# Loose softmax for the first quads, and masks on GpSimd, in a fused attention and feed-forward kernel

## The chip, the cores and the metric

The kernel runs on one core of one Trainium2 chip. Times are device microseconds of an execution; the profile is one execution taken by the hardware profiler. A core has a matrix engine (TensorE, PE in the profile, with its weight loads as PEld), VectorE (DVE), ScalarE (ACT), GpSimd (POOL) and SyncE (SP, which issues most transfers). The engines run side by side, each takes its own instructions in order, and they wait for each other by semaphores.

## The reference, cut to what matters

Attention over 8 batches of 8 heads, 576 rows and 64 columns a head, in which each row keeps only scores within tau = 0.02 of its maximum. Then a feed-forward layer whose hidden value is the largest of three products.

```python
scores = scale * np.matmul(q, k.transpose(0, 1, 3, 2))
thresh = np.max(scores, axis=-1, keepdims=True) - tau
scores = np.where(scores >= thresh, scores, -1000000000.0)
scores = scores - np.max(scores, axis=-1, keepdims=True)
attn = np.exp(scores)
attn = attn / (np.sum(attn, axis=-1, keepdims=True) + 1e-09)
x = np.matmul(attn, v)                      # then heads side by side: 4608 x 512
h = np.maximum(np.maximum(x @ w1, x @ w2), x @ w3)   # 512 -> 768
return h @ w_out                            # 768 -> 512
```

## The kernel before, in words

Four heads of one batch make a quad; there are 16. A quad's score rows are worked in 9 chunks of 128 rows by two heads, so that a chunk is a tile of 128 x 1152, made of two half tiles of 128 x 576. In all there are 144 chunks and 288 half tiles. q and k are loaded in float32, turned by TensorE (`transposed`, letter T), copied out by ScalarE (queries, letter a) and mostly VectorE (keys, letter c); a copy of the queries with the partition halves exchanged is made mostly by GpSimd (`swapped`, letter q).

For each half tile, `scores` (S) puts 576 columns into one of four slots of PSUM. `maximum` (m) on VectorE moves them to a tile z and takes each row's maximum with it. What follows depends on the half tile's digit in the table `MASKED` (line 24):

- 0: `threshold` (s) computes maximum minus tau on VectorE. `exponents` (e) on ScalarE applies a parametric ReLU that leaves scores below the threshold as they are and flattens those above by 2^-100. `numerators` (n) on ScalarE takes exp with the scale 2^100 and adds up the row. So ScalarE passes over the half tile twice.
- 1: ScalarE takes exp once (e), and VectorE compares, multiplies and adds up (`numerators`, letter k).
- 2 and 3: like 0 and 1, but ScalarE reads the scores from PSUM and not from z.

Then VectorE takes the reciprocal of both row sums (`reciprocals`, r), GpSimd multiplies z by it into the bfloat16 tile P (`normalized`, p, one half tile at a time), and SyncE issues a transposing transfer of P (`turned`, t). Once a quad's nine chunks are turned, `product` (O) multiplies by v: two pieces per quad, each for two heads, in tiles of 128 x 64 of the matrix engine, 20 matmuls a piece for an unsplit batch. One piece is copied out to x by VectorE (w), the other by ScalarE (x). v is cast to bfloat16 by GpSimd (`cast_v`, y).

The feed-forward part of a batch (`ffn`; F, with its second half as B) makes 18 hidden products, three for each of six blocks of 128 hidden columns. ScalarE copies out the first (h), VectorE takes the maximum with the others (v). Output products follow; their results are copied out (u, f, j) and stored (o, i, d). Weights are loaded (g) and cast by GpSimd (z). Batch 7 is worked in two parts (`SPLIT`, line 38).

No planner runs in the kernel. The string `ORDER` (line 40) gives the order: each letter issues one step, a digit behind S, T, O, F or N names the PSUM slot. `_Ordered` makes each engine keep that order. So a wait of one step holds back all later steps on its engine.

Of the kernel before, what the change touches and what calls it, by code (L numbers as in the profile page):

```python
# [24 lines left out]
220202110002002100110000100020020312000112012010100000000010100000001100  # L25
001000111010000101100000000000110001100000011110110200100000100010000000
110001101110100100010000001001100100000100101111102300000100100000001000
001000110100100001000000000100100001011110100011011100002100001000001013
# [7 lines left out]
PBUFS = 6  # L36

SPLIT = {7: ((0, 1), (2, 3, 4))}

ORDER = """  # L40
lllllllllT0laqqlcT1aS2lcqqgmS0S3lemS1lmnT2lmeS3lsaS0mnqlqemT3lyerclcapsnS1lS2eqmlS3qemznmS2perS1mnpsmnpT3ske
ytS1erkpT2agmnT3pclesqS2aqetS0meqlrnspmS1eqsT2nmpS3tnrcS0zlemS2eprmS3npmtS0npsgS1sermpS2emyS3eptmT0eplmS1ayl
meS0kynS2tssT3snkynkercperlT3pmnpmntqremS0lasprgeT3pmeS2psstnplnS0mzecesqrmS3etqkeS2gpnmS1npsmtnS0prmleS3pmS
2npsmnS0yrsmetperS2epmO1eqtnkplemnzswT2teS3rplS1empnmS3tpnssrS1klepS0mapermtS2epmT1S3nmqtnkO2qemncpS3txrskT1
peS2rmeS0ptmegpamS2npS1ertsmpnlkzS2elmS3eS0mpnlO1srkepsmnO2tyeprgwnpmT1xS3cpeS0sszmF2eS1meBqkF0ngqT3shrsmBay
S2tvpnF3rpemS1BpemF0pnsvT2BnyctS1esrlsT2mphS3lezS1maF0myntpT2sS3ngrcqF1eBmpnS2svpBnrmS3peS0tmeyF2zmnF3lBsvep
S0rhkBptesF2mgeS1zvF0nsmBpteBsrgvpnF1kS3phS2semBnqmF0S3evqF2ntrmBpelS1spvBnlmS3qhF0rsmepS1tnBpsmS3ezvS2eS1rm
pF0etsyO3mnlkngpO2eswetkBxrmpT3nF2rvpaS1BnqmS0hspS3meF2prS1smntBzesmF3ezvT0tBeclT1yS2pnvS0apsmtS3eyrmlS1epS2
mepF0mnqsmnS3tkBnkeF1restpkumeS2prtBumlperkpS0ustS2umS3pesmS1eqtT0mO2nlpceqsrmO3ntywelkS0pxlS1meF3prnS2smBye
myF0thpskS1oeBpF2nlvF3nlrmBpeBkpS1hstsvS0eF3lrmpnF2mBepBsveF1nT0vBtarkS3lhqS2smleF0prF1mnBysntBveS2plvnS0pom  # L50
F3nyS1pmeBsysmF0thT2rrlpeS1clF3epsmBnqT2svBaS1evqS2nmF0pS3nmqBtnmT2pS1hrcpS3esmS0petF2melS1rmpBnF3skpetF0sve
BlBmnF2vhtF1esrBkpnS0vtT3npBmS2arvpS0ermO3eqtsmepT1swntpS0cF2epesmtnS3kT1nS0mtBessrkpameS3preS1mS0uqmuS3mpnS
1tsmS2pnoS0rempS3lempO1lnkqlemO2lnymeO0srkpetkeF3swxykxpT2BercnprtS1uyS2upmF0termqS3eBymN2lhsskpelkS0eF3ertm
S1pjBlmeS0plvF2npS1mnyF3tpmnBsopT0nvBaS1kF2ieqrssmS0hlpBmelT1qF3snrvF0epcBlepS2vBnpsmtS1nS3rmphS2mnpF1smeS0B
snmF3tevS2T0mF1atBrsekpBevS0thS2pmF3nymS1qeBrsmnpS0tvF2eplF1rmnpBskeBptF3hsvS0eBrsstpmnS1lvT2qeO0mpnlscnT3wS
1etF2srramS0lnqBmlF3eqvT1nBcpS0thF2pemS1perS3mpBnmS0ptesO1smpnkteF3yvxT0BraktyS2esS1vpeS0mpnS3meqF2mnyrmpnT0
S1lceBqmeptrskS0pulS3muS1epmS2teF0rmplnskpeS1mtO3eklekO2esrmpesBknpwxS1kutS2urmopS3nF0myeS1mBetpsmF2hlS3rkep
BlmnF0S1prnsvT3tepBmF2apsssvS1eBtqmeS0qrS3hmtS1epsmF2lnpF0mleF3koBnBrvpeBstyvS1phsS2nmF3emS0nrS1tpmBnprS2smn
F0pveF1pBsremT3ptevBpS2chF0tnmF3ekBT1nvS2aBsmlnF0qvS1eS2rtrespmS3eBmqF1hmpT2nBcpS3ekpT2O0sasvterlmpO2ekqntwS
3xklpS1eF2ssmnF0yrBnmyS3evBptemS1plhS2ssmT3eyF0rcpeF1mBpntT3vnByS2ravpS0nmtpS3nsmS1eF2srmpektepS3slmnS0Bmeqn  # L60
mT1ktuS3urS0lcpeO2rlmpelmpeO3klpelweF1kqnsxS0rkepS2tmS3eBymemepS0kuF3quT2smeBtrF1kphoS0aBmnpS3tsN2rnvplnmpS1
erkpF0tjsF3mnBpsseBvS2ihrS1pmelS0mqeF3S2mnytBpmnoS1rF0eprsvF2ntpmBeBvqF1htskpS3esS0rmetS2pnmF3pBnmF0pesvT2te
BcF1nsBrvpntBskphT2F3erS0vlapBmnF1qvS2etpBmT0hS3rscpnF2lmS1qesS0sempBemS3yF1nvtS0nmBnT2ssrmpO3etspveF0wnS1rk
BpaS3tmhS2elqsF1mlS0qnmS3ermpBF2espsmS0npvBeS3tmeS1rvpO0ntmnsmS2yxS3empF0eskyerT1mpeS2cBtnypsmelkS3ulS2muS1e
smT0O3nsrplnpO2awetmeF3rkpxseT0S1ycntS2meF0poBrnsmpnkpF1ukBurS2shBqemF3oepvS0lS2nsmqF1emBptBnvF0hrrS2speS3mp
F1emBpntT2vepF3BssaktS0nvlBemS2hS1rsmptF0nS3mpeBmtnT2F1svnF3cetBBsrnvpS2hsrqS0meS1pmeT3F2sprmaS0npBmeF3ptsvn
S1qS0mnBtqmeS2yF1prevS0epssBmnS3qmS2htpmF0nlF1keBsmBertvO3pnvepF0serwpT2nBcpF3hktS1eBsrsmpnT0S2vtpaS1remqT3S
0nmyF2qectT1BpasmS3epvS1nS0mqnF2rmpemtpT3eS1keqS0smBercntpS1mupS3emF0ukessS1rmtpnBmopkS2uskS1eO3rukekO0yxeO3
ynwtprmopS0xmpS2emF3peS1mteBrsmpS0nF2pmhtS1nkBS3evF0nstmN2erkpeF1mBjpsBevS2hskF0eF3rkpteBmF1nBpveBkO2hsrvpeS
0rtwS1pnmF2npmS3eBympF1ntrvS0epBmpS2rF3svtpeS0mnpS1sBmiF2smhF0ntkBBervpS1etF3smpnF2BervpS1hsBpnmF0tevS3F1nmB  # L70
etrBkpO2vhO3nspS1xrwepS0mpF3smS2etF1snmBeBstvnS2S0veS3meF1snkeF2rmpnmpeBnkBerrptukpuO3rN1xpuO0jpuO3wptF1xpF2
hF0tvF1vF3hF0vtF1vF2hF0viF1vF2ohF0voF1vF3hF2vF1vF3hF2vO1vO0wF2xF3F1huF0vF3vF2ohF1vF3vF2hF0vF1vF3hF0vF2vF3hF1
vF2vF0hF1vF2vF0uF1ouN0ofjdi
# [31 lines left out]
def kernel(  # L105
# [44 lines left out]
    def weight_loads():  # L150


        def piece(dst, src):
            my = {}

            def load():
                my["t"] = stage.tile([128, 4 * 256], F32, name="stage")
                sync.dma_start(out=my["t"].rearrange("p (k f) -> p k f", k=src.shape[1]), in_=src)

            def cast():  # L160
                pool.tensor_copy(out=dst, in_=my["t"].rearrange("p (k f) -> p k f", k=src.shape[1]))
# [12 lines left out]
    zz = ctx.enter_context(tc.tile_pool(name="zz", bufs=ZBUFS))  # L174
    pp = ctx.enter_context(tc.tile_pool(name="pp", bufs=PBUFS))
# [68 lines left out]
    vrs = [one.tile([128, 4, D], BF16, name=f"vr{x}") for x in range(3)]  # L244

    def cast_v(L):
        L["vb"] = vp.tile([128, 4, 4, D], BF16, name="vb")
        pool.tensor_copy(out=L["vb"], in_=L["vm"])
        yield
        L["vrb"] = vrs[(2 * L["b"] + L["qd"]) % 3]  # L250
        for r in range(2):
            rows = slice(64 * r, 64 * r + 64)
            pool.tensor_copy(out=L["vrb"][rows, 2 * r:2 * r + 2], in_=Ls[2 * L["b"]]["vr"][rows, 4 * L["qd"] + 2 * r:4 * L["qd"] + 2 * r + 2])
# [93 lines left out]

    def masked(g, idx, r):
        return by_mask[2 * number[g, idx] + r] in "13"
# [37 lines left out]

    def numerators(c, r):
        z, acc = c["z", r], c["sm"][:, r:r + 1]
# [10 lines left out]
    def normalized(c):  # L400
        c["P"] = P = pp.tile([128, W], BF16, name="P")
        for n in range(2):
            pool.tensor_scalar(out=P[:, n * S:(n + 1) * S], in0=c["z", n],
                                    scalar1=c["rs"][:, n:n + 1], scalar2=1.0, op0=OP.mult, op1=OP.mult)
            if n:
                line["t"].append(c)
# [383 lines left out]
    x = 0  # L790
# [39 lines left out]
```

## Time and profile before

| | |
|---|---|
| median of 3 runs | 442.17 us (441.26 to 442.67) |
| span of the profiled execution | 440.2 us (its run time is not listed apart from the runs above) |
| busy PE, DVE, ACT, POOL | 418.9, 393.9, 403.6, 317.0 us |
| granted TensorE clock, mean | 0.988 |
| normalizations on POOL | 288 (250 from z tiles at 819 ns, 38 from stage tiles at 783 ns) |
| first feed-forward product starts | 71.3 us |
| last feed-forward maximum starts | 431.8 us |

In the group rows a line holds the engine, the operation, the tile written and those read, the shape, a count, the busy time and the mean of one. All recorded operations have the line of one helper, so groups are told apart by tile names: sc are scores in PSUM, z the half tiles in SBUF, th and nm the threshold and maximum of a row, rs the reciprocals, ptq the turned P, o the products, xt the attention output x, ph and po the hidden and output products, tp the turned q and k.

### The profile page before, as it was taken

How to read it: one execution, taken by the hardware profiler on the slowest of the kernel's cores; microseconds unless marked ns; L12 is line 12 of the kernel's file. 1: busy time of each engine (PE TensorE's matmuls, PEld its weight loads, DVE VectorE, ACT ScalarE, POOL GpSimd, SP SyncE). 2: the span in 40 equal slices, each digit the busy share in tenths (PEclk: the TensorE clock that was granted, in tenths of full speed). 3: DMA queues.
4: the chain of work that ended last, by engine and by line, in shares of the span. 5: the costliest groups of instructions: out<-in, count | busy, mean ns of one | idle time of the engine just before them, and what ended most of it. 6: DMA issues, size and time to landing. Idle time of an engine off the chain costs nothing.

```text
span 440.2 us, 14283 instructions
## 1 busy us (share of the span) xinstructions
PE 418.9 (95%) x5188; PEld 313.6 (71%) x5190; DVE 393.9 (89%) x1248; ACT 403.6 (92%) x834; POOL 317.0 (72%) x420
## 2 busy tenths in 40 slices
PE   7696789999999999999999999999999999999996
PEld 6353446787788776787678777887688777786873
DVE  4888899999999999999999999999889999998542
ACT  4999999999999999999999999999999998989521
POOL 1988999998787778867786778886585776554400
PEclk9987999999999999999999999999999999999999
DMA  6999999999999999999999999999698778583812
GB/s 190 276 239 214 270 215 260 263 252 252 220 277 224 237 165 242 291 160 232 189 242 238 202 182 273 192 199 208 135 237 153 147 109 185 102 169 72 192 50 85
DMA packets 213959, 88.50 MB, mean 201 GB/s; under 512 B 189184, under 2 KB 202240, under 8 KB 213888
## 3 DMA queue, kind: packets, MB, share of 16 engines
q1 hardware_dynamic: 213360, 86.96, 95.4%
q8 instruction: 41, 0.67, 0.6%
q10 hardware_dynamic: 528, 0.62, 0.5%
q14 instruction: 30, 0.25, 0.2%
HBM read 35.65 MB, written 9.44 MB: 102 GB/s over the span
## 4 chain that ended last, share of the span: by engine, by line
PE 78%; DVE 5%; POOL 5%; issue 4%; ACT 3%; DMA 2%; SPq 1%; DVEq 0%; POOLq 0%; ACTq 0%
PE ph L93 31%; PE sc L93 26%; PE po L93 10%; PE o L93 8%; POOL P L93 4%; PE tp L93 3%; ACT z L93 3%; DVE z L93 3%; DMA qm<-in_q_dram 2%; SPq L93 1%; DVE kt L93 1%; POOL w L93 1%; DVE stage L93 0%; DVE hm L93 0%; POOL qs L93 0%
## 5 line engine op out<-in xcount | busy, mean ns | idle before, releaser
L93 POOL TENSOR_SCALAR P<-z,rs 128x576 bf16<-128x576 f32 x250 | 202.0, 819 | 59.1 <-DVE rs L93 30.4
L93 DVE TENSOR_SCALAR_CACHE_REDUCE z<-sc 128x576 f32<-128x576 f32 x250 | 183.2, 749 | 12.2 <-PE sc L93 8.1
L93 PE MATMUL sc<-kt,qs 64*128 64x256 f32 (+2 forms) x640 | 179.8, 417 | 5.5 <-DVE z L93 3.9
L93 PE MATMUL sc<-kt,qt 64*128 64x320 f32 (+2 forms) x640 | 180.9, 429 | 3.1 <-DVE z L93 1.2
L93 PE MATMUL ph<-xt,w 64*128 64x288 bf16 (+2 forms) x2160 | 172.0, 283 | 0.2 <-DVE hm L93 0.2
L93 PEld LDWEIGHTS <-w 64*128 64x128 bf16 (+1 forms) x2160 | 128.0, 94 | 31.6 <-issue 4.0
L93 ACT ACTIVATE z<-z,th 128x576 f32<-128x576 f32 x161 | 120.5, 767 | 2.2 <-DVE th L93 1.9
L93 ACT ACTIVATE z<-z 128x576 f32<-128x576 f32 x175 | 117.6, 674 | 0.2
L93 PEld LDWEIGHTS sc<-kt,qs 64*128 64x128 f32 (+1 forms) x640 | 92.4, 179 | 22.5 <-DVE z L93 8.6
L93 PEld LDWEIGHTS sc<-kt,qt 64*128 64x128 f32 (+1 forms) x640 | 92.0, 179 | 14.7 <-DVE z L93 3.5
L93 DVE SCALAR_TENSOR_TENSOR z<-z 128x576 f32<-128x576 f32 x75 | 61.7, 827 | 1.4 <-ACT z L93 1.1
L93 POOL COPY qs<-qt 64x640 f32<-64x640 f32 (+3 forms) x66 | 45.9, 695 | 19.5 <-ACT qt L93 16.1
L93 ACT ACTIVATE z<-z,nm 128x576 f32<-128x576 f32 x72 | 53.9, 767 | 0.0
L93 PE MATMUL po<-wo,hT 64*128 64x512 bf16 (+3 forms) x454 | 53.3, 354 | 0.3
L93 DVE TENSOR_TENSOR hm<-ph,hm 128x576 bf16<-128x576 f32 (+2 forms) x54 | 37.0, 685 | 9.8 <-PE ph L93 9.6
L93 ACT ACTIVATE hm<-ph 128x576 bf16<-128x576 f32 (+2 forms) x54 | 31.9, 590 | 14.3 <-PE ph L93 13.8
L93 PEld LDWEIGHTS <-hT 64*128 64x128 bf16 (+2 forms) x456 | 28.4, 95 | 18.5 <-issue 2.6
L93 DVE TENSOR_TENSOR hT<-ph,hm 128x576 bf16<-128x576 f32 (+2 forms) x54 | 36.9, 683 | 2.8 <-PE ph L93 1.0
L93 PE MATMUL o<-ptq,vb 128*64 128x512 bf16 (+2 forms) x544 | 38.7, 282 | 0.2 <-DVE z L93 0.2
L93 POOL TENSOR_SCALAR P<-stage,rs 128x576 bf16<-128x576 f32 x38 | 29.5, 783 | 11.7 <-DVE rs L93 8.4
L93 ACT ACTIVATION_READ_ACCUMULATOR z<-z 128x1 f32 x175 | 33.6, 192 | 0.0
L93 PEld LDWEIGHTS <-vb 128*64 128x64 bf16 x544 | 22.4, 111 | 14.0 <-issue 5.6
(44 smaller groups left out, 412.2 us busy)
## 6 DMA issues: line engine op xcount, KB each, us to landing
vm<-in_v_dram SPq DMA_DIRECT2D x32, 256.0 KB, 4.6
qm<-in_q_dram SPq DMA_DIRECT2D x15, 512.0 KB, 4.7
km<-in_k_dram SPq DMA_DIRECT2D x15, 512.0 KB, 5.4
out_dram<-ob SPq DMA_DIRECT2D x14, 512.0 KB, 4.5
stage<-in_moe_w_dram SPq DMA_DIRECT2D x9, 512.0 KB, 5.6
ptq<-P SPq DMA_TRANSPOSE x144, 4.5
vr<-in_v_dram SPq DMA_DIRECT2D x16, 128.0 KB, 3.8
stage<-in_moe_w_out_dram SPq DMA_DIRECT2D x3, 512.0 KB, 5.5
```

The lines of the kernel that those rows point to most:

```text
L93: ins = fn(*a, **kw)
```

## The change

It has four parts, and a new order text.

- **Loose quads.** For the first three quads (`LOOSE = 3`), exp or the mask writes straight to P in bfloat16, without row sums, reciprocal and normalization. Instead TensorE makes a third product per quad with a matrix of ones in the place of v, which gives each head's row sums on 32 partitions. ScalarE takes their logarithm (L) and the exponential of its negative (E). VectorE multiplies both product pieces by that on the way to x (`scaled`, on w).
- **Masks on GpSimd.** 34 half tiles have the digit 4. After `threshold`, GpSimd computes (threshold minus score) times 2^100 and writes it as a saturated int8 into the high byte of a bfloat16 tile (`marked`, b): a huge number where the score is below the threshold, nothing or minus zero elsewhere. GpSimd adds this to z (`moved`, C), and ScalarE takes exp once (G). 13 of them lie in the first three quads.
- **Products in 32-column tiles.** A piece now holds the even or odd columns of all four heads, in four tiles of 128 x 32, 40 matmuls a piece for an unsplit batch. v is cast in that layout, and the rows of the hidden weights are loaded in the matching order, in two transfers each.
- **Buffers.** v has two buffers instead of three, P keeps six, now as named tags, one mark tile is added, the 9th-row output tile is shared with the logarithms, and the activation set with log and exp is asked for at the start.

Digits 0 to 4 of the table: 187, 84, 14, 3, 0 before and 162, 80, 10, 2, 34 after.

```diff
-MASKED = """ 2202021100020021001100001000200203...
+MASKED = """ 4201042142001321424220142114041004...
-ORDER = """ lllllllllT0laqqlcT1aS2lcqqgmS0S3lem...
+ORDER = """ lllllllllllT1lT0aclqqacqqS1lS2lmS0l...
+FARS = 1
+LOOSE = 3
+FAR = 2.0 ** 100
...
+                    for qd in range(2):
+                        sync.dma_start(out=my["t"].rearrange("p (qd j f) -> p qd j f", qd=2, j=2)[:, qd], in_=src[:, qd])
...
-                yield piece(t[:, :, cols], w[:, cols].rearrange("(ko p) f -> p ko f", p=128))
+                yield piece(t[:, :, cols], w[:, cols].rearrange("(qd p j) f -> p qd j f", qd=2, j=2))
...
-    vp = ctx.enter_context(tc.tile_pool(name="vp", bufs=3))
+    vp = ctx.enter_context(tc.tile_pool(name="vp", bufs=2))
...
-        pool.tensor_copy(out=L["vb"], in_=L["vm"])
+        pool.tensor_copy(out=L["vb"].rearrange("p h c j d -> p (h c) j d"),
+                         in_=L["vm"].rearrange("p h c (d j) -> p (h c) j d", j=2))
...
+        if on_pool(c, r):
+            if loose(c["g"]):
+                scalar.activation(out=part_of(c, r), in_=z, func=AF.Exp, bias=c["nm", r], scale=-1.0)
+            else:
+                scalar.activation(out=z, in_=z, func=AF.Exp, bias=c["nm", r], scale=-1.0, accum_out=summed(c)[:, r:r + 1])
+            return
...
+    def marked(c, r):
+        c["far", r] = t = far[next(fars) % FARS]
+        pool.tensor_scalar(out=t.bitcast(mybir.dt.int8).rearrange("p (n x) -> p n x", x=2)[:, :, 1],
+                           in0=c["z", r], scalar1=c["th", r], scalar2=FAR, op0=OP.add, op1=OP.mult)
+
+    def moved(c, r):
+        pool.tensor_tensor(out=c["z", r], in0=c["z", r], in1=c["far", r], op=OP.add)
...
+        if loose(c["g"]):
+            if masked(c["g"], c["idx"], r):
+                vector.scalar_tensor_tensor(out=part_of(c, r), in0=z, scalar=thr, in1=z, op0=OP.is_ge, op1=OP.mult)
+            else:
+                scalar.activation(out=part_of(c, r), in_=z, func=AF.Exp, scale=-1.0 / FLAT)
+            return
...
-                for i in range(2):
-                    w = vb[:, 2 * r + i, (1, 3, 0, 2)[m], :] if m < 4 else vrb[:, 2 * r + i, :]
-                    tensor.matmul(ps[64 * i:64 * i + 64, p0:p0 + n], w,
+                for h in range(4):
+                    r, i = divmod(h, 2)
+                    if j is None:
+                        w = ones[2 if m < 4 else r]
+                    else:
+                        w = vb[:, h, (1, 3, 0, 2)[m], j, :] if m < 4 else vrb[:, h, j, :]
+                    tensor.matmul(ps[32 * h:32 * h + 32, p0:p0 + n], w,
...
+        def logs():
+            L["rec", part] = hp_.tile([128, S], F32, name="ob9", bufs=1)
+            scalar.activation(out=L["rec", part][:, 0:hi - lo], in_=source(), func=AF.Ln)
+
+        def inverses():
+            t = L["rec", part][:, 0:hi - lo]
+            scalar.activation(out=t, in_=t, func=AF.Exp, scale=-1.0)
+
+        def scaled():
+            vector.tensor_tensor(out=dest(), in0=source(), in1=L["rec", part][:, 0:hi - lo], op=OP.mult)
...
+    if LOOSE:
+        scalar.preload_act_table_set("natural_log_exp_and_others")
...
-                    for r in range(2):
-                        yield product(Ls[g], r, x_of, part)
+                    for j in (None, 0, 1) if loose(g) else (0, 1):
+                        yield product(Ls[g], j, x_of, part)
```

More of the change, by code (lines that the diff above doesn't have):

```diff
@@ L74 @@
+d
 """
@@ L242, in load @@
                 yield
-    vrs = [one.tile([128, 4, D], BF16, name=f"vr{x}") for x in range(3)]
+    vrs = [one.tile([128, 4, 2, D // 2], BF16, name=f"vr{x}") for x in range(3)]
     def cast_v(L):
-        L["vb"] = vp.tile([128, 4, 4, D], BF16, name="vb")
-        pool.tensor_copy(out=L["vb"], in_=L["vm"])
+        L["vb"] = vp.tile([128, 4, 4, 2, D // 2], BF16, name="vb")
+        pool.tensor_copy(out=L["vb"].rearrange("p h c j d -> p (h c) j d"),
+                         in_=L["vm"].rearrange("p h c (d j) -> p (h c) j d", j=2))
         yield
@@ L400, in normalized @@
     def normalized(c):
-        c["P"] = P = pp.tile([128, W], BF16, name="P")
+        c["P"] = P = paper(c)
         for n in range(2):
@@ L413, in turned, with product @@
         sync.dma_start_transpose(out=L["pt"][:, :, c["idx"] * 128:(c["idx"] + 1) * 128], in_=c["P"])
-    def product(L, r, target, part=None):
+    ones = [one.tile([128, D // 2], BF16, name=f"ones{x}") for x in range(3)]
+    vector.memset(ones[2], 1.0)
+    for x in range(2):
+        vector.memset(ones[x], 1.0)
+        vector.memset(ones[x][64 - 64 * x:128 - 64 * x], 0.0)
+    def product(L, j, target, part=None):
         pt, vb, vrb = L["pt"], L["vb"], L["vrb"]
@@ L678, in chunks @@
             made.append(c)
+            if not loose(g):
+                tight.append(c)
             yield c
@@ L753, in issue @@
         elif what == "s":
-            threshold(*line["s"].pop(0))
+            c, r = line["s"].pop(0)
+            threshold(c, r)
+            if on_pool(c, r):
+                line["b"].append((c, r))
+        elif what == "G":
+            exponents(*line["G"].pop(0))
+        elif what == "b":
+            c, r = line["b"].pop(0)
+            marked(c, r)
+            line["C"].append((c, r))
+        elif what == "C":
+            c, r = line["C"].pop(0)
+            moved(c, r)
+            line["G"].append((c, r))
         elif what == "e":
@@ L757, in issue @@
             exponents(c, r)
[L758 removed]
+            if True:
+                line["k" if masked(c["g"], c["idx"], r) else "n"].append((c, r))
         elif what in "nk":
             c, r = line[what].pop(0)
[L761 to L764 removed]
             numerators(c, r)
         elif what == "r":
[L767 removed]
+            c = tight[line["r"].append(0) or len(line["r"]) - 1]
             assert c["summed"]
```

164 lines of the change are left out of this document (91 added, 73 removed).

## The prediction

> **What bounds the kernel now.** I read the page's busy times and slices first, then the chain, then windows cut at the first matrix product of the feed-forward part (71.3 us), then waits, then the instruction groups ahead of that cut.
>
> ```profile
> span 440.2 us, 14283 instructions
> PE 418.9 (95%) x5188; PEld 313.6 (71%) x5190; DVE 393.9 (89%) x1248; ACT 403.6 (92%) x834; POOL 317.0 (72%) x420
> PE   7696789999999999999999999999999999999996
> ACT  4999999999999999999999999999999998989521
> PE 78%; DVE 5%; POOL 5%; issue 4%; ACT 3%; DMA 2%; SPq 1%; DVEq 0%; POOLq 0%; ACTq 0%
> ```
>
> PE is full except at both ends; ACT is full from the second slice on. So two different bounds follow one another. The windows (length, then busy us and count of PE, PEld, DVE, ACT, POOL, then granted clock and DMA) part them:
>
> ```profile
> 0.00:8.40 8.40, 6.47 (x69) 5.73 (x71) 2.48 (x11) 2.38 (x4) 1.73 (x8) 1.00 0.59 149
> 8.40:71.30 62.90, 48.51 (x436) 28.11 (x434) 55.45 (x188) 62.00 (x132) 56.29 (x74) 0.92 1.14 246
> 71.30:85.00 13.70, 13.13 (x184) 9.95 (x182) 12.47 (x41) 13.37 (x30) 12.61 (x19) 1.00 1.18 265
> 85.00:400.00 315.00, 314.60 (x4145) 244.03 (x4147) 302.98 (x961) 307.71 (x630) 240.01 (x314) 1.00 1.01 204
> 400.00:440.20 40.20, 36.16 (x365) 25.74 (x363) 20.50 (x52) 18.12 (x41) 6.30 (x8) 1.00 0.39 101
> ```
>
> ```profile
> PE ph L93 <- DVE hm L93: 0.2, 1, 0.2
> ```
>
> From 8.4 to 71.3 ACT is busy 62.00 of 62.90 us and PE only 48.51, at a clock of 0.92: softmax paces, PE starves. From 85 to 400 PE is busy 314.60 of 315.00, and the single wait above is all it has there: PE paces. So work taken from ACT after 85 us buys nothing; what counts is when PE becomes full, and that is near the first feed-forward product.
>
> **The first stretch, engine by engine.** Groups from 0 to 71.3 us (count, then total busy us, mean ns, idle before):
>
> ```profile
> L93 ACT ACTIVATE z<-z 128x576 f32<-128x576 f32 x36 | 24.2, 674 | 0.0
> L93 ACT ACTIVATE z<-z,th 128x576 f32<-128x576 f32 x26 | 19.6, 767 | 0.6 <-DVE th L93 0.3 <-DVE rs L93 0.2
> L93 ACT ACTIVATE z<-z,nm 128x576 f32<-128x576 f32 x12 | 9.2, 766 | 0.0
> L93 ACT ACTIVATE z<-sc,nm 128x576 f32<-128x576 f32 x12 | 8.7, 728 | 1.3 <-DVE z L93 1.3
> L93 ACT ACTIVATION_READ_ACCUMULATOR z<-z 128x1 f32 x36 | 6.9, 193 | 0.0
> L93 ACT ACTIVATE qt<-tp 128x640 f32<-128x640 f32 (+3 forms) x10 | 5.4, 542 | 2.2 <-PE tp L93 1.9 <-DVE kt L93 0.2
> L93 ACT ACTIVATE xt<-o 128x576 bf16<-128x576 f32 x2 | 1.3, 631 | 0.0
> L93 DVE TENSOR_SCALAR_CACHE_REDUCE z<-sc 128x576 f32<-128x576 f32 x53 | 38.7, 751 | 6.7 <-PE sc L93 4.2 <-POOL P L93 2.3
> L93 DVE SCALAR_TENSOR_TENSOR z<-z 128x576 f32<-128x576 f32 x12 | 10.0, 843 | 0.3 <-ACT z L93 0.2
> L93 DVE COPY kt<-tp 128x640 f32<-128x640 f32 (+3 forms) x9 | 5.8, 650 | 0.0
> L93 DVE TENSOR_SCALAR th<-nm 128x1 f32<-128x1 f32 x28 | 3.8, 146 | 0.1
> L93 DVE RECIPROCAL rs<-sm 128x2 f32<-128x2 f32 x23 | 3.6, 158 | 0.8 <-ACT z L93 0.7
> L93 POOL TENSOR_SCALAR P<-z,rs 128x576 bf16<-128x576 f32 x46 | 35.8, 791 | 3.0 <-DVE th L93 1.4 <-POOL vr L93 0.9
> L93 POOL COPY qs<-qt 64x640 f32<-64x640 f32 (+3 forms) x16 | 10.3, 646 | 9.4 <-ACT qt L93 8.7
> L93 POOL CAST w<-stage 128x1024 bf16<-128x1024 f32 x6 | 6.7, 1120 | 0.1
> L93 POOL CAST vb<-vm 128x1024 bf16<-128x1024 f32 x3 | 3.1, 1035 | 0.1
> L93 POOL CAST vr<-vr 64x128 bf16<-64x128 f32 x5 | 3.0, 600 | 0.1
> ```
>
> Instructions overlap, so a mean is more than what each takes from its engine. The timeline (start, length) gives the step from one start to the next:
>
> ```profile
> 51.30 0.77 ACT L93 ACTIVATE z<-z,nm 128x576 f32<-128x576 f32 x1
> 51.96 0.68 ACT L93 ACTIVATE z<-z 128x576 f32<-128x576 f32 x1
> 52.53 0.20 ACT L93 ACTIVATION_READ_ACCUMULATOR z<-z 128x1 f32 x1
> 52.63 0.73 ACT L93 ACTIVATE z<-sc,nm 128x576 f32<-128x576 f32 x1
> 53.25 0.78 ACT L93 ACTIVATE z<-z,th 128x576 f32<-128x576 f32 x1
> 51.79 0.75 DVE L93 TENSOR_SCALAR_CACHE_REDUCE z<-sc 128x576 f32<-128x576 f32 x1
> 52.58 0.15 DVE L93 TENSOR_SCALAR th<-nm 128x1 f32<-128x1 f32 x1
> 52.65 0.75 DVE L93 CAST xt<-o 128x576 bf16<-128x576 f32 x1
> ```
>
> ACT: biased exponential or flattening 0.66, plain exponential 0.57, reading its sum 0.10, flattening from PSUM 0.62; other ACT groups are taken at mean less 0.10. DVE: group mean less 0.07 or 0.08, so maximum 0.68, threshold 0.07.
>
> **The sum to the first feed-forward product.** I count the letters of the order text ahead of its first F, old against new, and the mask kinds among them.
>
> ACT. Old: 38 first passes from SBUF x 0.66 + 12 from PSUM x 0.62 + 36 second passes x (0.57 + 0.10) + query copies 4.4 + 2 product copies x 0.53 = 62.1, against 62.00 busy. New: 29 x 0.66 + 9 x 0.62 + 24 x 0.57 (loose, no sum) + 13 exponentials behind GpSimd's marks x 0.66 + 4.4 + 2 logarithms x 0.53 + 2 exponentials x 0.57 = 53.6. Less 8.5.
>
> DVE. Old: 53 maxima x 0.68 + 28 thresholds x 0.07 + 12 masks x 0.76 + 23 reciprocals x 0.08 + 9 key copies x 0.57 + 2 product copies x 0.67 = 55.4. New: 55, 32, 11, none, 10 and 4 of these (scaling with a PSUM and an SBUF operand at the 0.67 of the cast) = 56.4, less the old first stretch's small extras: I set DVE as unchanged, 55.45.
>
> POOL. Old 56.29. It loses 46 normalizations (35.8) and 2 weight casts (2.2), gains 2 swaps (1.3), one v cast (1.0), one remainder cast (0.6) and 13 mark-and-add pairs. No row shows either half of a pair. The mark's nearest row is the normalization, also one tensor in with a column and a constant: 0.79; bounds 0.65 (the swap's mean) and two such passes, 1.58. The add has two tensors in: bounds one pass, 0.79, and three, 2.37; I take one and a half, 1.2, since a second operand has to be read but nothing more is written. A pair 2.0 (1.4 to 3.95), 13 make 26: POOL 47.2.
>
> The Trainium skill (GPSIMD Engine Reference, Performance versus the Vector engine) gives 4497 ns for a two-tensor add of 2048 columns and explains it by one shared read port; by length that is an estimate of 1.26 for 576 columns, and the pair would be 2.05. No run here shows it yet.
>
> So the leader changes from ACT (62.0) to DVE (55.45), with ACT at 53.5 and POOL at 47 close behind. A leader with a close second reaches less than 100%: between 85 and 400 DVE runs 302.98 of 315.00, 96%, beside ACT. 55.45/0.96 = 57.6 against 62.9: the first feed-forward product comes at 66.0 instead of 71.3. Gain 5.3; at ACT's old 98.6% it would be 6.7, at DVE's old 88% nothing.
>
> **The rest.** Ahead of that product the new order has issued 57 half scores instead of 54 and 6 products instead of 4, so behind it stand 3 half scores fewer and 33 products instead of 32; the feed-forward pieces are the same 320. These nearly cancel, if a product of four 32-column tiles costs what one of two 64-column tiles does. The old one:
>
> ```profile
> 248.01 1.18 PE L93 MATMUL o<-ptq,vb 128*64 128x512 bf16 x16
> 249.27 1.16 PE L93 MATMUL o<-ptq,vb 128*64 128x512 bf16 x16
> 409.87 0.32 PE L93 MATMUL o<-ptq,vb 128*64 128x64 bf16 x8
> ```
>
> A product starts 1.26 us after the one before, 20 matmuls. The new one has 40 over as many streamed columns, 31 ns each. Eight short ones pass in 0.32 us, 40 ns each with their latency in it, so that the issue rate alone doesn't forbid 31. Bounds 1.26 (four at once) and 2.5 (two at once); I take 1.26. The two extra products before the cut lie in PE's idle time (62.90 - 48.51); the third costs 1.3, and the three half scores pay for it.
>
> Behind the cut ACT has 22 first passes and 17 summed second passes fewer and 21 summed exponentials more: -14.5 - 11.4 + 16.0 = -9.9. DVE has 4 masks fewer, -3. POOL gains 21 pairs, 18 of them behind 85 us by their place in the mask table: 240 + 36 = 276 of 315, 88%. PE has no wait there that these would shorten.
>
> Edits at nothing: weight loads split in two, 9 more issues on SP, and behind them the transposes; SP has the time, it waits for POOL's P alone as long as
>
> ```profile
> SPq L93 <- POOL P L93: 124.0, 86, 5.1
> ```
>
> and loose P tiles come from ACT and DVE sooner. Without that cover each issue delays a transpose. The strided v cast has the same elements. Two v buffers instead of three: POOL's cast then waits for products two quads back, with swaps and normalizations queued behind it; the order places it at least one half score after them. One mark tile: mark and add share an engine in order. A loose P tile must be free before ACT or DVE writes it, where POOL had that wait; six tiles cover it, if transposes lag more, ACT stalls with all exponentials behind it. The activation set is loaded once in both.
>
> Sum: 440.2 - 5.3 + 0 = 434.9. The profiled span lies 2.0 below the median 442.17, which I carry over: 437.
>
> **The rivals.**
> (a) GpSimd becomes the leader; slower. Besides pairs POOL has 21.2 in the first stretch, so it leads above (57.6 - 21.2)/13 = 2.8 us per pair. At the upper bound, 3.95: 72.6, product at 81.0, 9.7 later; 85 to 400 would stand at 311 of 315. Time 452. For: POOL already holds 56.29 of 62.90. Against: the near rows put the pair at 2.0.
> (b) The column tiles run two at a time, 2.5 us a product: 33 x 1.24 less some shorter ones of the last batch, some +36, less 5.3: 473. It eats the gain from 0.16 us per product on. For: 40 matmuls a product were never shown; against: the short matmuls above. The Trainium skill (TensorE: Matmul & The Clock Gate, Wait — 56ns, not 53.3ns?) names 62 ns per matmul as the issue cost in one decode setting; 40 of them would be 2.48 us, the same time. The row of eight in 0.32 us speaks against it, though eight could have been queued ahead.
> (c) DVE stays at 88% since it waits on scores or a late P, and nothing is gained: 442.
> (d) PE, which waits 0.2 us now, waits behind 85 us for POOL at 88%: each wait adds in full; at 2% of 315 that is 6.3, and 443.
>
> **How the numbers follow.** Forecast 0.62, (a) 0.14, (b) 0.08, (c) 0.08, (d) 0.08. Within 0.3% (1.3 us, about what this measurement can tell) are most of (c) and half of (d): same 0.11; slower: (a), (b), the rest of (d) and (c): 0.27. The forecast's own range runs from 431 (98.6% for DVE, and a cleaner start) to 440. The range that leaves out (b) and little of (a) is 430 to 452.
>
> **What would show it.** First feed-forward product near 66 us; DVE near 96% and ACT below it ahead of that; POOL pair near 2.0; a product of 40 matmuls in 1.26; PE still without waits from 85 to 400, ACT there near 298. A pair above 2.8, a product above 1.4, or PE waiting on P would make it wrong.

## The result, and the profile after

The changed kernel takes 464.02 us (median, 463.4 to 464.72) beside 441.94 for the kernel before in the same comparison: ratio 1.0497, 95% interval 1.0478 to 1.0517. It is 22 us slower where 5 us less was forecast. The profiled execution has a span of 461.6 us; before it had 440.2.

First the head of the page, the slices and the chain of the changed kernel:

```profile
span 461.6 us, 15782 instructions
PE 430.6 (93%) x5988; PEld 309.8 (67%) x5990; DVE 405.4 (88%) x1216; ACT 389.7 (84%) x772; POOL 351.4 (76%) x434
PE   7677785999979999999999999999999999999996
ACT  2999794799969989999999998899899998987422
PE 72%; DVE 6%; DMA 6%; issue 3%; POOL 2%; ACT 2%; SPq 1%; POOLq 0%; DVEq 0%; ACTq 0%
```

ScalarE is no longer full in the first third, as meant. But DMA holds 6% of the chain, where it held 2%, and both engines have holes up to the 12th slice. The windows, cut as those of before, with the new first feed-forward product at 70.4 us (length, then busy us and count of PE, PEld, DVE, ACT, POOL, then clock and DMA):

```profile
8.40:70.40 62.00, 48.52 (x615) 30.10 (x617) 58.66 (x165) 53.53 (x85) 47.39 (x55) 1.00 1.15 223
70.40:85.00 14.60, 9.38 (x106) 7.81 (x104) 8.08 (x19) 8.04 (x14) 8.26 (x9) 0.77 1.00 231
85.00:400.00 315.00, 309.65 (x4464) 227.07 (x4463) 296.27 (x912) 293.49 (x604) 273.26 (x339) 1.00 1.03 201
```

The first stretch ends 0.9 us earlier than before, and right behind it lies a hole of 14.6 us in which every engine is idle for a third to nearly half of the time, while the transfers run as in the other stretches (DMA 1.00). From 85 to 400 TensorE has 5 us of idle time where it had 0.4. The waits of the changed kernel (total, times, longest):

```profile
PEld sc L96 <- DVE z L96: 12.7, 17, 3.5
POOL w L96 <- DMA stage<-in_moe_w_dram: 9.1, 4, 3.8
PE tp L96 <- DVE z L96: 7.2, 5, 5.2
PE sc L96 <- DVE z L96: 5.0, 5, 3.1
ACT P L96 <- POOL w L96: 4.3, 1, 4.3
POOL P L96 <- DMA ptq<-P: 3.5, 1, 3.5
ACT P L96 <- DMA ptq<-P: 2.6, 1, 2.6
```

GpSimd's casts wait for weight blocks, writers of P tiles wait for transposes (the row that names GpSimd's cast for ScalarE is one of these too, as is shown below), and TensorE waits for slots that VectorE empties late. The first of these rows is no new one over the whole execution (it was 12.0 us before); it is new behind 85 us. From 85 to 400 us, before and after:

```profile
PEld sc L93 <- DVE z L93: 1.4, 5, 0.3
PEld sc L96 <- DVE z L96: 8.4, 12, 3.5
```

TensorE's longest wait, 5.2 us up to 78.3 us, is the hole. Its row names VectorE; a load of queries on which the same step waits, asked for at 73.12, landed just ahead of that, at 78.18, so which of the two held it longer can't be told.

The records of the row maxima show where the time is lost. Start of the n-th of the 288 on VectorE, in us; the last column is the run with a quarter of the weight bytes, told below:

```
maximum   before   after   difference   small weights
 54         71.9     67.5      -4.4         64.5
 72         96.7    104.3      +7.6         93.4
 90        120.7    133.5     +12.8        121.7
144        198.1    211.0     +12.9        199.1
216        299.3    317.0     +17.7        305.2
287        404.5    424.7     +20.2        412.9
```

A second account needs no positions. Behind its first feed-forward product TensorE has the same to stream in both kernels: at 2.4 columns per ns (the trace has 122 to 123 ns from one hidden product of 288 columns to the next, which is 2.35), float32 counted twice and matmuls in tiles side by side once, 341.3 us before and 341.1 after. But from there to its last matmul pass 364.7 us before (71.3 to 436.0) and 386.6 after (70.4 to 457.0). So the whole loss is idle time of TensorE between equal work. The rate, a little too high, makes the idle time of both kernels larger by the same amount. The gaps, sorted by whether the tile shape changes (into or out of a product's or a ninth chunk's tiles) and by length:

```
gaps behind the first F    short, shape changes   short, others   over 0.35 us   all us
before                       60, 10.7 us           10.1             2.7          23.4
after                        97, 16.2 us           14.5            15.1          45.8
small weights                97, 16.2 us           12.9             6.7          35.8
small weights, grouped       67, 11.6 us           15.6            19.4          46.6
before, products split       67, 11.6 us            9.4            13.8          34.9
```

### The profile page after: what moved, and what is told of

The parts are those of the page before. It is cut to its first block, busy times and chain, and to the rows that moved or that the text cites. A ratio compares the mean times of both kernels' runs of the same rounds, so it can differ in the third digit from the quotient of the medians.

```text
span 461.6 us, 15782 instructions
## 1 busy us (share of the span) xinstructions
PE 430.6 (93%) x5988; PEld 309.8 (67%) x5990; DVE 405.4 (88%) x1216; ACT 389.7 (84%) x772; POOL 351.4 (76%) x434
## 4 chain that ended last, share of the span: by engine, by line
PE 72%; DVE 6%; DMA 6%; issue 3%; POOL 2%; ACT 2%; SPq 1%; POOLq 0%; DVEq 0%; ACTq 0%
PE ph L96 29%; PE sc L96 24%; PE po L96 9%; PE o L96 7%; DMA ptq<-P 4%; DVE z L96 3%; PE tp L96 3%; DMA stage<-in_moe_w_dram 1%; POOL P L96 1%; DVE stage L96 1%; ACT z L96 1%; ACT P L96 1%; SPq L96 1%; POOL w L96 0%; DVE kt L96 0%
## 5 line engine op out<-in xcount | busy, mean ns | idle before, releaser
L96 PE MATMUL sc<-kt,qt 64*128 64x320 f32 (+2 forms) x640 | 184.5, 425 | 9.0 <-DVE z L96 4.2
L96 PE MATMUL sc<-kt,qs 64*128 64x256 f32 (+2 forms) x640 | 183.6, 415 | 4.7 <-ACT z L96 1.5
L96 POOL TENSOR_SCALAR P<-z,rs 128x576 bf16<-128x576 f32 x196 | 160.4, 830 | 35.7 <-DVE rs L96 14.3
L96 ACT ACTIVATE z<-z,th 128x576 f32<-128x576 f32 x140 | 105.0, 765 | 7.1 <-DVE th L96 7.0
L96 ACT ACTIVATE z<-z 128x576 f32<-128x576 f32 x122 | 82.0, 673 | 0.2
L96 ACT ACTIVATE z<-z,nm 128x576 f32<-128x576 f32 x85 | 64.5, 765 | 0.8 <-DVE z L96 0.7
L96 DVE SCALAR_TENSOR_TENSOR z<-z 128x576 f32<-128x576 f32 x56 | 51.2, 920 | 0.0
L96 ACT ACTIVATE hm<-ph 128x576 bf16<-128x576 f32 (+2 forms) x54 | 32.0, 592 | 17.0 <-PE ph L96 16.2
L96 POOL TENSOR_TENSOR z<-z,far 128x576 f32<-128x576 f32 x31 | 42.1, 1358 | 2.0
L96 PE MATMUL o<-ptq,vb 128*32 128x64 bf16 (+2 forms) x1088 | 38.4, 280 | 0.0
L96 POOL TENSOR_SCALAR far<-z,th 128x576 int8<-128x576 f32 x31 | 24.8, 798 | 14.2 <-DVE th L96 10.2
```

The source lines that it names most:

```text
L96: ins = fn(*a, **kw)
```

## The experiments

The diffs are shortened: `...` and the comment lines stand for what is left out.

**Parts of the change in the changed kernel's order.** Three runs first: GpSimd's pairs replaced, the weights at their old places, and both.

```diff
 # e2: a pass of ScalarE in the place of the mark, no add, second exponential at G
-        pool.tensor_scalar(out=t.bitcast(int8)...[:, :, 1], in0=c["z", r], scalar1=c["th", r], scalar2=FAR, ...)
+        scalar.activation(out=z, in_=z, func=AF.Prelu, bias=c["th", r], scale=1.0, alpha=FLAT)
-        pool.tensor_tensor(out=c["z", r], in0=c["z", r], in1=c["far", r], op=OP.add)
 # e3: ORDER: letters g and z moved to the row maximum behind which they stand in the old order
 # e4: e2 and e3
```

> The changed kernel with the 34 pairs on GpSimd taken out: the mark becomes the flattening pass of ScalarE in the same place, the add is dropped, and the later exponential becomes the second pass. Theory G (GpSimd's pairs cost through the port that VectorE's mask shares, and through a fuller GpSimd): the mask on VectorE falls back from 0.92 to about 0.83 us, and 8 us or more of the 22 come back, although ScalarE has 21 us more work. Theory W (late weight loads hold up GpSimd and with it everything at 66 to 82 us): the time stays within 3 us of the changed kernel or gets worse, as ScalarE has more to do.

> The changed kernel with its weight loads and casts moved to the places they have in the order before, counted in row maxima. Theory W: GpSimd's waits for the weight transfers (9.1 us) vanish, the hole at 70 to 85 us closes, and about 10 us of the 22 come back. Theory G: the hole is refilled by GpSimd's own work, and less than 3 us come back.

> Both at once: no pairs on GpSimd, and weights at the places of the order before. If both theories hold and are independent, the gains of the two runs add up and the time comes within 5 us of the kernel before or below it; if one cause feeds the other, the sum is less than the two.

Measured: e2 465.23 (1.0517, 1.0477 to 1.0557), e3 460.64 (1.0428, 1.0379 to 1.0477), e4 465.21 (1.0504, 1.0447 to 1.0562). Putting ScalarE's pass in the place of the pairs gives nothing, so theory G falls (it said 8 us or more). The old places for the weights give 3.4, between what the two theories said, and together with e2's edit nothing is left of that (e4). In e3 the hole shrinks, but the first feed-forward product comes at 76.5. The wait on weights moves with the rest rather than going; in e2 and e3:

```profile
POOL w L96 <- DMA stage<-in_moe_w_dram: 14.1, 5, 5.9
```

```profile
POOL w L96 <- DMA stage<-in_moe_w_dram: 6.5, 2, 3.7
```

**Parts of the change in the old order.** The old order with 32-column tiles, the weights in two transfers and the strided cast (e1), and from there, with one P tile fewer so that all fits in memory (e8, the control), the loose quads (e6), the pairs (e7) and both (e5).

```diff
 # e1, from the changed kernel: old MASKED and ORDER
-FARS = 1, LOOSE = 3, vp bufs=2
+FARS = 0, LOOSE = 0, vp bufs=3
 # e8, from e1
-PBUFS = 6
+PBUFS = 5
 # e6, from e8: LOOSE = 3 (r and p of the first quads left out of ORDER; third pieces, L and E put in)
 # e7, from e8: FARS = 1, the 34 digits 4 put into the old MASKED, b, C and G into ORDER
 # e5, from e8: both
```

> The kernel before with its own masks and order, but products in four 32-column tiles, the weight rows in the matching order and loaded in two transfers each; no loose quad, no mask on GpSimd. If column tiles ran two at a time or were held up by issue (rival b), a product would take above 1.4 us and the time would rise by 5 us or far more. If they run four at a time, as the profile of the changed kernel suggests (two products of 40 matmuls in 2.56 us), the time stays within 2 us of the kernel before.

> Control for the next three: the order and masks of the kernel before, 32-column products, weights in two transfers, three v buffers, and five P tiles instead of six to make room. Products in 32 columns alone took 446.4 us. If the sixth P tile matters (transposes that lag), the time rises by 3 us or more over that; otherwise it stays within 1.5 us of 446.

> The control plus the first three quads loose, in the old order, with no mask on GpSimd. ScalarE has 54 row sums less to read (5 us) and 1.6 us of product copies less, GpSimd 54 normalizations less. Theory O (the new order costs, not the parts): the first feed-forward product comes 3 us or more earlier than in the control and the time is 2 to 4 us below it. Theory P (the parts cost): the time is at or above the control.

> The control plus the 34 pairs on GpSimd, placed where the old order had the first pass, no quad loose. ScalarE loses about 20 us of work, GpSimd gains 34 x 2.1 = 71 us less nothing, so that it holds about 388 us. Theory O: the time stays within 3 us of the control. Theory P: GpSimd and VectorE's masks hold each other up, VectorE's mask mean rises from 0.83 to above 0.9 us, and the time rises by 5 us or more.

> The control plus both parts, in the old order. Theory O: at or below the control, near 444, so 18 us or more of the changed kernel's 22 come back by the old order alone. Theory P: 455 or more, as in the changed kernel.

Measured: e1 446.36 (1.0097, 1.0062 to 1.0131), e8 453.58 (1.0259, 1.0236 to 1.0282), e6 456.65 (1.0328, 1.0288 to 1.0368), e7 503.23 (1.1363, 1.1322 to 1.1404), e5 487.58 (1.1018, 1.0968 to 1.1068). So the new tiles, cast and transfers cost 4.5 without any of the other parts, and one P tile less costs 7.2 more. The wait on P's transposes, in e1 and in e8:

```profile
POOL P L96 <- DMA ptq<-P: 2.3, 3, 1.6
```

```profile
POOL P L96 <- DMA ptq<-P: 10.6, 8, 2.3
```

Loose quads, which take 54 normalizations from GpSimd, make it 3.1 slower, and the pairs 49.7, since in an order not made for them ScalarE stands behind GpSimd; in e7:

```profile
ACT z L96 <- POOL z L96: 55.5, 26, 4.1
```

So these three runs show what the parts cost in an order that wasn't made for them, not what they cost in the new one. For the pairs e11 and e17 below tell that. No run takes the loose quads out, or the third v buffer back, alone in the new order, so their own cost there isn't known.

**Are the transfers the cause?** A quarter of each weight block, in one transfer, in the changed kernel and in the kernel before.

```diff
-                    for qd in range(2):
-                        sync.dma_start(out=my["t"]...[:, qd], in_=src[:, qd])
+                sync.dma_start(out=my["t"][:, 0:256], in_=w[0:128, cols])
-                pool.tensor_copy(out=dst, in_=my["t"]...)
+                pool.tensor_copy(out=dst, in_=my["t"][:, 0:256].unsqueeze(1).broadcast_to([128, 4, 256]))
```

> The changed kernel, with only a quarter of each weight block loaded (128 rows of 1 KB in one transfer) and used four times by GpSimd's cast, so that the hidden and output products are computed with wrong weights; all engines do the same instructions as before that. Theory T (transfers): from 55 to 105 us the queue that carries the transposes of P and the weights is full, GpSimd's 9.1 us wait for weight blocks and the hole at 70 to 85 us come from it, and most of the 10.6 us lost between the 54th and the 72nd row maximum. Then the wait is gone, the first feed-forward product comes at about 66, the 72nd maximum at about 97, and the time is about 454. Rival O (the order and the engines' own work set it): the wait goes, another takes its place, 461 to 464.

> Control: the kernel before with the same quarter of the weight blocks. Theory T: the kernel before has only 2.6 us of waits on transfers, so it gains little: 439 to 442. If it gains as much as the changed kernel does (5 us or more), transfers bound both and explain none of the difference.

Measured: 450.7 (1.0191, 1.0157 to 1.0225) and 441.89 (0.9991, 0.9982 to 1.0001). The changed kernel gains 13.3 us and the kernel before nothing that can be measured, so 13.3 of the 22 hang on the weight transfers. The first feed-forward product comes at 68.2 and the 72nd maximum at 93.4 (theory T said 66 and 97). The hole is closed; the windows of this run:

```profile
8.40:68.20 59.80, 49.07 (x615) 30.46 (x615) 57.91 (x166) 54.80 (x87) 48.72 (x56) 0.97 1.10 229
70.00:85.00 15.00, 14.93 (x223) 11.55 (x219) 14.42 (x41) 15.00 (x30) 14.29 (x16) 1.00 1.02 172
85.00:400.00 315.00, 311.72 (x4496) 229.81 (x4492) 294.32 (x914) 293.06 (x604) 272.09 (x340) 0.99 0.99 192
```

How the hole comes about is seen in the changed kernel's timeline around it:

```profile
64.52 1.75 SPq L96 DMA_DIRECT2D stage<-in_moe_w_dram  x2
66.45 5.99 SPq L96 DMA_TRANSPOSE ptq<-P  x2
68.56 1.28 POOL L96 TENSOR_TENSOR z<-z,far 128x576 f32<-128x576 f32 x1
72.51 1.04 POOL L96 CAST w<-stage 128x1024 bf16<-128x1024 f32 x1 [2.67 <-DMA stage<-in_moe_w_dram]
73.58 0.78 ACT L96 ACTIVATE P<-z,nm 128x576 bf16<-128x576 f32 x1 [4.25 <-POOL w L96]
74.39 0.76 DVE L96 TENSOR_SCALAR_CACHE_REDUCE z<-sc 128x576 f32<-128x576 f32 x1 [2.65 <-ACT P L96]
```

Two things are late here. A weight block is asked for at 64.52, and its cast on GpSimd, which the order places where the block was expected, starts at 72.51. And ScalarE's exponential waits 4.25 us, with VectorE's next maximum behind it. The row names GpSimd's cast, but the exponential needs nothing of it: the add for its half tile, ahead of the cast, had ended at 69.84. The exponential belongs to the 25th chunk and writes the P tile that the 19th held (there are six), and it also waits on the semaphore of that chunk's transpose. That transpose is the first of the two issued from 66.45 on; by the trace's record it landed at 73.50, 7.05 us after its issue. So the transfers hold ScalarE by a late transpose, not by a late cast. With small weights the same exponential starts 0.43 us behind its add, without a wait.

**One transfer or two.** In the old order (e12, from e1) and in the new (e15), the same bytes, with the rows of the weights in the old order.

```diff
-                    for qd in range(2):
-                        sync.dma_start(out=my["t"]...[:, qd], in_=src[:, qd])
+                    sync.dma_start(out=my["t"]..., in_=w[:, cols].rearrange("(ko p) f -> p ko f", p=128))
```

> The first experiment (old order and masks, products in 32-column tiles, weights in two transfers, strided cast of v, 446.4) with each weight block loaded in one transfer in the old order of rows, so that the feed-forward products meet wrong rows. If the 4.3 us of that experiment come from the second transfer, 442; if from the smaller column tiles and the strided cast, 446.

> The changed kernel with each weight block loaded in one transfer in the old order of rows (the same bytes; the feed-forward products meet wrong rows). The run with a quarter of the weights gained 13.3 us; it had fewer bytes and also one transfer instead of two. If the second transfer is what costs, this run gains most of that, about 453; if the bytes in a short time are, it stays at 461 to 464. In the old order the same edit gave 1.4 us.

Measured: 444.96 (1.0055, 1.0038 to 1.0073) and 457.9 (1.0376, 1.0328 to 1.0424). The second transfer costs 1.4 in the old order (the intervals of e1 and e12 overlap), and 6.1 in the new, between what the two theories said. So of the 13.3 that small weights give, some 6 go with the second transfer and, if the two add, some 7 with the bytes. In the old order 2.9 of e1's 4.5 stay with one transfer; the tiles and the strided cast are what is left to cost that, and no run parts these two. Half a block lands little sooner than a whole one. The weight transfers of the changed kernel and of e15 (count, size, median us to landing):

```profile
stage<-in_moe_w_dram SPq DMA_DIRECT2D x18, 256.0 KB, 5.4
```

```profile
stage<-in_moe_w_dram SPq DMA_DIRECT2D x9, 512.0 KB, 6.0
```

In the old order these are 4.1 (e1) and 5.5 (e12); around the hole, from 55 to 85 us in the new order, 6.0 and 6.1. A cast needs both halves, and the second is issued after the first.

**Pairs and products with ones, without the transfers in the way.** The pairs left out of the changed kernel (e11), and with small weights (e17); the products with ones cut short (e16).

```diff
 # e11 and e17: the bodies of marked() and moved() are empty
 # e16, from the run with small weights
-            for m, (*q0, p0, n) in order:
+            for m, (*q0, p0, n) in (order if j is not None else [x for x in order if x[0] == 0]):
-            scalar.activation(..., in_=source(), func=AF.Ln)
+            scalar.activation(..., in_=source(), func=AF.Copy)
```

> The changed kernel without GpSimd's marks and adds: the 34 half tiles go through one exponential unmasked (wrong rows there), GpSimd does 73 us less, and no engine does anything in its place. Theory P (the pairs cost time: VectorE's two-operand masks stretched to 3.7 us beside them, P tiles late behind them, PE waiting for z): the row maximum 90 comes 3 or more earlier, and the time is about 457. Rival: the pairs are hidden, as in the earlier run in which a pass of ScalarE took their place and the time stayed at 465: 463 to 465, and what is lost is lost by the loose tiles, the transfers and the order.

> The run with a quarter of the weights, and GpSimd's marks and adds left out as well (34 half tiles unmasked). If the pairs cost nothing once transfers are out of the way: 450 to 451. If they cost as much as in the changed kernel (2.5): 448. If GpSimd was the next bound: 445 or less.

> The run with a quarter of the weights (450.7), and in it the three products with ones cut to their first fifth (8 matmuls for 40) and the logarithm replaced by a copy, so that the first three quads are scaled wrongly. TensorE does 3.1 us less. Theory PE (behind 58 us TensorE paces, so its work counts in full): about 447.6. Rival (the three products lie in idle time ahead of the first feed-forward product, as the prediction had it for two of them): 450 to 451.

Measured: e11 461.48 (1.0425, 1.0404 to 1.0446), e17 450.11 (1.0204, 1.0162 to 1.0246), e16 452.03 (1.0244, 1.0194 to 1.0294). The pairs cost 2.5 beside the slow transfers; without them 0.6, which can't be told from nothing (the intervals overlap). The products with ones cost nothing that can be told (450.7 with them). Both theories of a cost there fall. One row of e17 answers the forecast directly. Without pairs and with few transfers its first feed-forward product comes at 66.3:

```profile
8.40:66.30 57.90, 49.47 (x614) 30.49 (x616) 56.34 (x164) 54.09 (x87) 22.32 (x32) 0.97 1.11 229
```

So here the first product comes when it was forecast, and the time is still 450.1 and not 437: 13 us of the miss lie behind that product.

**The order of TensorE's work.** With small weights 8.6 us remain. The new order text goes into and out of a product's tiles more often (35 stretches, 22 before). One run groups such letters (e18, from small weights), one splits them in the kernel before (e19).

```diff
 # e18: ORDER, 16 letters S and O moved forward, each with its slot; TensorE's letters at one place
-S1S2O3S0T1O3O2S0
+S1S2O3O3O2S0T1S0
 # e19: old ORDER, 10 second pieces O moved two TensorE steps back; TensorE's letters at one place
-O1O2O0F3T2B
+O1O2F3T2O0B
```

> The run with a quarter of the weights, with 16 letters of the order text moved forward, so that pieces of one quad's product and the two half scores of the ninth chunk follow each other on TensorE without other work between them: stretches of products 35 to 26 (22 in the order before), of ninth-chunk scores 24 to 18 (18). Nothing else is changed. Theory M (TensorE loses 0.14 to 0.21 us at each step between tiles of 64 x 128 and tiles of 128 x 32 or 64 x 64, some 0.35 for a stretch): 15 stretches fewer, about 5 us, 445.5. Rival (these gaps are hidden, or the moved letters wait for their slot or transposes): 450 to 453.

> The kernel before with one edit in its order text: at 10 of the quads the second piece of the product is issued two TensorE steps later (with the letter that copies it out moved behind it), so that TensorE goes into and out of the product's tiles 10 times more, 32 stretches instead of 22. All work is the same. Theory M (a change of tile shape costs TensorE 0.14 to 0.21 us, two to a stretch): 3.0 to 3.5 us slower, 445.3. Rival (the gaps are filled or the records mislead): 441.5 to 442.5. If moved letters make others wait, more than 447.

Measured: e18 465.31 (1.0538, 1.0516 to 1.056), e19 455.82 (1.031, 1.0293 to 1.0327). Grouping was expected to gain 5 and lost 14.6; ten splits were expected to cost 3.3 and cost 13.6. The table of gaps parts the two effects. The changes of shape do what theory M says: 30 fewer short ones in e18 take 4.6 us off, 0.15 each. But the long gaps grow from 6.7 to 19.4 in e18 and from 2.7 to 13.8 in e19. The cause that I find in the order texts is the edit itself: the moved letters kept their slots, so steps that go into the slot which the step just ahead has filled, and must wait until it is copied out, rose from 1 to 7 in e18 and from 1 to 10 in e19 (`O3O3` above is one). That is 2.1 and 1.2 us of long gaps for each. The trace of e19 bears this out: nine of its long gaps lie right behind a product, and seven of these end with a product's copy to x. So these two runs show what a change of shape costs and what a slot taken too early costs; what the same grouping would give with slots dealt anew was not tried. The kernel before and the changed one have one such step each, so this is not where the changed kernel's own time went. In e18 TensorE's weight loads wait for slots, from 85 to 400 us; in e19 ScalarE waits for products to copy out:

```profile
PEld sc L96 <- DVE z L96: 13.4, 13, 2.7
```

```profile
ACT xt L93 <- PE o L93: 10.0, 8, 2.4
```

**Are the two gains at the weights one?** One transfer, and loads and casts at their old places.

```diff
 # e20, from e15: ORDER with letters g and z at the row maximum behind which the old order has them
```

> The changed kernel with each weight block in one transfer (457.9 alone) and the loads and casts of weights at the places that they have in the order before, counted in row maxima (460.6 alone, with two transfers); the feed-forward products meet wrong rows. If the two gains add, 454.5; if they are the same gain, since both only take pressure from the transfers between 60 and 85 us, 457 to 460.

Measured: 459.93 (1.0409, 1.0364 to 1.0454), no better than one transfer alone. By these intervals the two gains do not add; both are gains at the same place.

No version beat the kernel before. The nearest that computes the same is e1, at 446.36.

## Why the prediction was wrong, point by point

**Two successive bounds.** The reading of the kernel before holds, and the two engines named for the first stretch hit: ScalarE 53.6 forecast and 53.53 measured, GpSimd 47.2 and 47.39.

**The first feed-forward product at 66.0.** It came at 70.4. The step that failed is the term for VectorE, "unchanged, 55.45": it was busy 58.66, at 95% of the stretch, close to the 96% taken. One part of that is my own: the count gave 56.4, and I took it down to 55.45 for "small extras", though the same count of the old stretch (55.4 of 55.45) leaves none. The other part is the masks: the 11 of the stretch took 12.5 us; the sum has 8.4 for them, with some 0.08 taken off each for overlap. Small weights bring the product to 68.2 (masks 11.8), leaving the pairs out as well to 66.3 (masks 9.8), with VectorE at 56.34. So of the 4.4 us missed, 2.2 hang on the weight transfers and 1.9 on the pairs, and the count of letters was right.

**The pair at 2.0 us.** Right within a tenth; the add and the mark on z tiles:

```profile
L96 POOL TENSOR_TENSOR z<-z,far 128x576 f32<-128x576 f32 x31 | 42.1, 1358 | 2.0
L96 POOL TENSOR_SCALAR far<-z,th 128x576 int8<-128x576 f32 x31 | 24.8, 798 | 14.2 <-DVE th L96 10.2 <-DMA ptq<-P 1.3 <-ACT P L96 0.9
```

1.36 and 0.80 make 2.16. Rival (a), GpSimd as leader, falls: it was busy 273 of 315 behind the cut (276 forecast). The estimate for the add that I worked out from the Trainium skill (GPSIMD Engine Reference, Performance versus the Vector engine), 1.26, was nearer to the 1.36 than my 1.2.

**The product of 40 matmuls at 1.26 us.** Right; two follow each other at 1.23 us, and rival (b) falls:

```profile
131.28 1.16 PE L96 MATMUL o<-ptq,vb 128*32 128x512 bf16 x32
132.51 1.15 PE L96 MATMUL o<-ptq,vb 128*32 128x512 bf16 x32
```

**The rest: equal work, and "PE has no wait there".** The first half is right (341.3 and 341.1 us to stream), the second is the step that made the forecast wrong by its sign. That TensorE waited 0.2 us before was a property of the old order text. I carried it over to another text without a term. The row was also read for more than it says: the profile models the end of a matmul (a hidden product is listed with 283 ns and the next starts after 122 to 123), so 314.60 busy of 315.00 us can hold short gaps, and the count by columns has 23.4 us of idle time behind the first feed-forward product before. Measured are 22.4 us more: 12.4 in long waits, 5.5 in more changes of tile shape, 4.4 in other short gaps. Of the long waits the hole has 5.2, and one wait behind a mask 3.1 (below). Rival (d) comes nearest, with 0.08 and 6.3 us: it has TensorE waiting behind 85 us, but for a GpSimd at 88%. e17 takes 39 us of work off GpSimd there (272 to 233) and is no faster by more than its noise, so that load isn't the cause, and the size is missed by more than three times. With small weights 12.4 us more idle time than before is left, of which 3.1 is set off by the earlier first product. By the gaps, changes of tile shape are 5.5 of it, and e18 bears out their price; the other 6.8 (35.8 less 23.4 less 5.5, rounded) are gaps of which I know the cause of one: 2.2 us behind such a mask again. The rest stays open.

**Edits at nothing.** Three of them were not. For the split weight loads I named SP's idle time as the cover, and said that each issue without it delays a transpose; priced by e15 the second transfer is 6.1 of the 22. The old places for the loads are worth 3.4 by e3, but by e20 nothing on top of one transfer. For the loose P tiles I named the very wait (transposes that lag, ScalarE stalled with all exponentials behind it) and put it at nothing, since "six tiles cover it". It came: 4.25 us in the hole, and 2.6 in the row that names the transpose. That six tiles leave no reserve is seen in the old order too, where one tile less costs 7.2. And the strided cast of v, with the same elements, takes 1.23 us where the plain one took 1.09 (mean of 16); its share in e12's 2.9 us isn't known.

**The masks on VectorE** were counted at their old length. Next to a queue of GpSimd work one can take far longer; from the timeline of the changed kernel:

```profile
126.08 3.72 DVE L96 SCALAR_TENSOR_TENSOR stage<-stage 128x576 f32<-128x576 f32 x1
126.30 2.90 POOL L96 TENSOR_SCALAR P<-z,rs 128x576 bf16<-128x576 f32 x4
129.73 0.75 DVE L96 TENSOR_SCALAR_CACHE_REDUCE z<-sc 128x576 f32<-128x576 f32 x1
130.54 0.53 PE L96 MATMUL sc<-kt,qt 64*128 64x320 f32 x1 [3.09 <-DVE z L96]
```

A mask that has a mean of 0.92 us on z tiles here lasts until four normalizations in a row have ended, and TensorE's next score waits 3.09 us for the maximum behind it. The same meeting stands in the other runs of the new order: 3.73 us in e2, 3.03 in e3, 3.05 with small weights (where the next score waits 2.18), 3.58 in e17. In the kernel before no mask took over 1.43. So this wait belongs to the new order text, with or without the pairs, and not to the transfers. The Trainium skill (SBUF — State Buffer, SBUF: two separate sides) calls the port pair of the two engines an exclusive lock, taken by whoever starts first, for the whole instruction. That agrees in kind. One instruction would be a wait of some 0.8; in this row the mask ended only behind four in a row.

## What to carry to other kernels

A kernel whose order is written out to a fraction of a microsecond has little free engine time, and a new order text has a cost of its own: ten letters moved without a change of work took 13.6 us, most of it since steps then took a slot that was still full. So price the order, not only the work. Before an engine's relief is counted, ask what its next step will wait for besides engines: a buffer taken earlier waits for the transfer that empties it, and a transfer split in two, or late, comes out as a wait there. A high DMA row alone doesn't tell this: it stood at 1.14 and 1.18 before, and there fewer weight bytes gave nothing. Where TensorE "has no waits", count its columns, its steps between tile shapes and the slots that it needs. And where a row names an engine whose work the step doesn't use, look for a transfer that landed then.

## What the runs showed of the hardware

- Products in four tiles of 128 x 32 run at the pace of two of 128 x 64 (1.23 us for 40 matmuls, 1.26 for 20 before).
- Each change between tile shapes left a gap of 0.15 to 0.18 us on TensorE, by the reckoning of the table of gaps (10.7 us for 60, 16.2 for 97, 11.6 for 67). The Trainium skill (TensorEngine Tiling (Array Packing), Key Properties) says that a change of tiling mode drains the engine; the gaps agree with that, though what fills them can't be seen here.
- A weight transfer of 256 KB took over two thirds of the time of one of 512 KB to land (medians 5.4 and 6.0 us in the new order, 4.1 and 5.5 in the old one).
- A mask with two operands in SBUF on VectorE lasted 3.72 us beside four GpSimd normalizations in a row, and 3.73, 3.03, 3.05 and 3.58 in four other runs of that order.
